# Splitting z of the first batch on GpSimd, with split scores from half step 6 and a half-wide diagonal half in the second chunk

## The chip, the cores and the metric

The kernel runs on one core of one Trainium2 chip. The core has engines that work side by side, each through its own queue of instructions in order: TensorE (PE in the profile; PEld is its loading of weights), VectorE (DVE), ScalarE (ACT), GpSimd (POOL), and SyncE (SP), which here issues all DMAs. They share the on-chip memory SBUF; PE writes its results to PSUM. The metric is the device time of one execution in microseconds (us), the median over several runs.

## The reference

Two stages, of which the change touches the first. For each of 8 batches with 2496 tokens, `u` and `v` have 256 columns and `z` has 64:

```python
scores = scale * np.matmul(z, z.transpose(0, 2, 1))   # scale = 1 / 2496
attn = np.maximum(scores, 0.0) ** 2
out = np.matmul(attn, v)
x = u * out
```

The scores are symmetric, which the kernel uses. The second stage, a mixture of experts with soft routing (slots of 8 experts filled by a softmax over all tokens, two small layers for each expert, and a second softmax that spreads the results back), takes `x` as its input.

## The kernel before

**Tiles.** The tokens of a batch are cut into 5 blocks (0 to 4) of up to 512. A chunk is the 512 queries of one block; its sums over all keys build up in PSUM (`acc`). A chunk goes through the 5 blocks of keys in the order that `MEETS` gives it (`FIRST_MEETS` for the first batch), each in two halves of 256 keys, so it has 10 half steps. The list `halves` holds all half steps of all batches, numbered from 0.

**One half step.** `scores` multiplies keys by queries on PE. `prepare` takes the result through ACT (`Relu`, then `Square`, tile `r`), and splits it in two parts, `ph` (rounded to the fast matmul format fp32r) and `pl` (what the rounding left, a subtraction on DVE). The sums are three products: `v` high with `ph`, `v` low with `ph`, `v` high with `pl`. The loop (lines 865 to 895) runs the sums of half step `h` while it prepares half step `h + 2` (from half step 18 on, `h + 3`).

**Scores, raw and split.** A raw score takes z in 32 bits as it was loaded: two matmuls, which PE works off in several passes. A split score takes z as a high and a low part (`zt`) and needs six matmuls in fp32r (line 293). Half steps below `RAW_SCORES` use raw scores. The raw z of batch 0 lies in `cw` until it is no longer needed.

**Splitting z.** `load_z` (line 103) starts the DMA of one block and returns `split`: twice a cast of 64x512 and a subtraction of 64x512. In the first batch `z_splits` holds these functions, and the loop runs them at its end (line 893) after half steps 8 to 11, as `FIRST_Z` says. Block 0 isn't split, since in half steps 0 to 9 its scores are raw and later ones are taken turned. `open_loads` issues the loads of z and v in a fixed order while a ring of four raw v tiles has room; blocks 0, 1 and 2 are issued before the loop, 3 during `prepare_first`, 4 in the loop at half step 1.

**Turned half steps.** Where a pair of blocks has met before with the roles exchanged, its scores are not computed again: at the first meeting DVE transposes `r` into `y` (32x32 blocks), `store` writes `y` to DRAM, and `fetch` reads it back rearranged. Such a half step is `turned` and goes without scores, `Relu` and `Square`. On the diagonal (a block with itself) a half can be borrowed likewise: an entry such as `(1, 0)` in `MEETS` names a single half; one with part 2 lends its transposed second half (`lend`), and the one with part 3 computes scores for only half of its queries and gets the other half from DRAM (`borrow`). In `FIRST_MEETS` the second chunk, `(1, 0, 2, 4, 3)`, has no such halves: half steps 10 and 11 are the whole diagonal, 12 and 13 are turned, 14 to 19 are blocks 2, 4 and 3.

**Order of work.** The wrapper `InOrder` pins every instruction of PE, ACT, DVE and SP behind the one written before it on its engine. Instructions that don't go through it, those of `constants` and the no-operation below, are placed by a planner where they fit.

**The no-operation on GpSimd.** When half step `h + 2` has scores to compute, the sums of `h` are cut into two phases with the scores between them. The two phases write the two halves of `acc` crosswise, and phase 1 must not begin before phase 0 has ended:

```python
if phase == 0:
    turn = nc.gpsimd.nop()   # line 484
    await_(turn, mm)
    return turn
```

The no-operation waits for the last matmul of phase 0, and the first matmul of phase 1 waits for the no-operation. Beside these GpSimd has only `constants` at the start (lines 164 to 179) and two instructions near the end (lines 916 and 918).

Of the kernel before, what the change touches and what calls it, by code (L numbers as in the profile page):

```python
# [37 lines left out]
MEETS = (  # L38
# [3 lines left out]
)  # L42
FIRST_MEETS = ((0, 1, 2, 3, 4), (1, 0, 2, 4, 3)) + MEETS[0][2:]

FIRST_Z = {8: 1, 9: 2, 10: 4, 11: 3}

RAW_SCORES = 12

PAD = 224

# [1 line left out]
def f32(ap):  # L52
    return ap.bitcast(F32)
# [14 lines left out]
def attn_soft_moe_kernel(ctx, tc, uT, v, zz, phi, ww, outT):  # L68
    nc = tc.nc

    pe, act, dve, sp = (InOrder(tc, x) for x in (nc.tensor, nc.scalar, nc.vector, nc.sync))

    def pool(st, name, n, side=None):
        return st.enter_context(
# [28 lines left out]
    def load_z(b, j):  # L103
        if b == 0:
            raw = cw[:, 19 + 4 * j : 23 + 4 * j].rearrange("p g n -> p (g n)")
        else:
            raw = raws.tile([P, 512], F32, tag="raw", name=f"zr_{b}_{j}", bufs=NRAW)
        sp.dma_start(raw, zz[b, :, j * 512 : (j + 1) * 512])
        zraw[b, j] = raw

        def split():
            t = zt[b, j]
            for h in (1, 0):
                rows = HALF[h]
                act.copy(t[rows, h], raw[rows])
                dve.tensor_sub(t[rows, 1 - h], raw[rows], f32(t[rows, h]))

        return split

# [19 lines left out]
    z_splits, v_splits = {}, []  # L139
# [24 lines left out]
    def constants():  # L164
        make_identity(nc, ident)


        nc.gpsimd.memset(rsel, 0.0)
        for h in range(4):
            rows = slice(h * NS, (h + 1) * NS)  # L170
            nc.gpsimd.tensor_copy(ssel[rows], ident[rows, rows])
        for h in range(2):
            for r in range(4):
                nc.gpsimd.tensor_copy(
                    rsel[:, h, r, 16 * h : 16 * h + 16].rearrange("k (j s) -> k j s", s=SE),
                    ident.rearrange("k (j q) -> k j q", q=NS)[:, :, 0:SE],
                )
        sp.dma_start(phi_sb, phi.rearrange("(c p) s -> p c s", p=P))
        nc.gpsimd.memset(one, 1.0)
# [11 lines left out]
    def chunks(b):  # L191
        if b < B - 1:
            return [(j, 0, min(QC, S - j * QC), b * S + j * QC) for j in range(NQ)]
        t0 = b * S
        out = [(NQ - 1, 0, ROT, t0)]
        out += [(j, 0, QC, t0 + ROT + j * QC) for j in range(NQ - 2)]
        j = NQ - 2
        return out + [(j, o, QC // 2, t0 + ROT + j * QC + o) for o in (0, QC // 2)]
# [20 lines left out]
    for b in range(B):  # L219
        for ch, meets in zip(chunks(b), MEETS[b == B - 1] if b else FIRST_MEETS, strict=True):  # L220
            order = []
# [18 lines left out]
    def run(todo):  # L240
        now, todo[:] = todo[:], []
        for f in now:
            f()
# [17 lines left out]
    def scores(k, ps=None, cut=slice(None)):  # L261
# [22 lines left out]

        if k < RAW_SCORES:
            for h, rows in enumerate(HALF):
# [168 lines left out]
    def sums_halves(k, acc, phase, before):  # L455


        x = halves[k]
        todo = [[], []]
        hi, lo = pend[k]  # L460
        for t, kt in enumerate(x.tiles):
            vt = vt_[x.b, kt // 2][:, kt % 2]
            hh, lh, hl = (vt[:, 0], hi[:, t]), (vt[:, 1], hi[:, t]), (vt[:, 0], lo[:, t])
            if kt < KT - 1:
                for h in range(2):
                    todo[h] += [hh, lh, hl]
            else:

                todo[0] += [hh] if phase else [hh, lh]
                todo[1] += [hl] if phase else [lh, hl]  # L470
        for i in range(len(todo[0])):
            for h, rows in enumerate(HALF):
                vp, pp = todo[h][i]
                c = h ^ phase ^ side[0]
                mm = pe.matmul(
                    totals(acc, c, x), vp[rows, c * P : (c + 1) * P], columns(pp[rows], x),
                    start=(x.begins and phase == 0 and i == 0),
                    stop=(x.ends and phase == 1 and i == len(todo[0]) - 1),
                )
                if before is not None:  # L480
                    await_(mm, before)
                    before = None
        if phase == 0:
            turn = nc.gpsimd.nop()
            await_(turn, mm)
            return turn
        side[0] ^= 1

    def sums_whole(k, acc):

        x = halves[k]
        hi, lo = pend[k]
        for t, kt in enumerate(x.tiles):
            assert kt < KT - 1
            vt = vt_[x.b, kt // 2][:, kt % 2]
            for c in range(2):
                for i, (l, r) in enumerate(((0, hi), (1, hi), (0, lo))):
                    pe.matmul(
                        totals(acc, c, x), vt[:, l, c * P : (c + 1) * P], columns(r[:, t], x),
                        start=(x.begins and t == 0 and i == 0),  # L500
                        stop=(x.ends and t == 1 and i == 2),
                    )
# [270 lines left out]
    def weights(left):  # L773

        if left in W_TAKES:
            W_TAKES[left]()
        for i in W_LOADS.get(left, ()):
            load_w(i)
# [26 lines left out]
    def transfers(h):  # L805

        x = halves[h]
        if x.at == 2:
            load_u(x.b, x.ch)
        for k in range(h + 1, min(h + 9, len(halves))):  # L810
            y = halves[k]

            if y.turned and y.opens and k not in arriving and k not in fetched:
                if k - h <= 7 and (y.b, y.p, y.ch[0]) in scratch:
                    fetched.add(k)
                    fetch(k)
            if y.borrows and k - h <= 5 and k not in fetched and (y.b, y.p, y.p) in scratch:
                fetched.add(k)
                borrow(k)
        for f, b, i in splits.get(h + 2, ()):  # L820
            if (b, 0) not in vt_:
                take_blocks(b)
            landing.setdefault(h + 2, []).extend([f(b, i)] if f is load_z else f(b, i))
        while stores and stores[0][0] <= h + 1:
            stores.pop(0)[1]()

    def split_first_v():
        if v_splits:
            for f in v_splits.pop(0):
                f()  # L830
            open_loads(NRAW)
# [3 lines left out]
    def between_last(k):  # L835

        if k:
            if k == 1:
                xps.append(sc_ps.tile([P, 2, QC], F32, tag="sc", name="tr_first"))
                two = [raws.tile([P, 2, D], F32, tag="raw", name=f"xt_last_{i}", bufs=NRAW) for i in range(2)]  # L840
                xt_last.extend(t[:, i] for t in two for i in range(2))
            ps = xps[0][:, k - 1, 0:D]
            turn_x(ps, xg_[NQG - 1], k - 1)
            copy_x(act.copy, ps, xt_last[k - 1])
# [16 lines left out]
    prepare(1)  # L861
    keep_busy(2)
    constants()
    acc = None
    for h, x in enumerate(halves):
        if x.begins:
            acc = acc_ps.tile([P, 2, QC], F32, tag="acc", name=f"acc_{x.ch[3]}")
        last = len(halves) - h
        transfers(h)
        weights(last)  # L870
        for f in landing.pop(h, ()):
            behind.append(f)
        if work and (x.at > 1 or last <= 20):
            work.pop(0)()
        ahead = [k for k in range(h + 2 + (h > CATCH), h + 3 + (h >= CATCH)) if k < len(halves)]
        split_first_v()
        if ahead and not halves[ahead[0]].turned:
            turn = sums_halves(h, acc, 0, None)
            prepare(ahead.pop(0))
            sums_halves(h, acc, 1, turn)  # L880
        else:
            if ahead and not x.ends:
                prepare(ahead.pop(0))
            elif not ahead:
                run(middle)
                run(behind)
                between_last(3 - last)
            sums_whole(h, acc)
        if x.ends:
            finish_chunk(x.b, x.ch, acc)  # L890
        for k in ahead:
            prepare(k)
        if h in FIRST_Z:
            z_splits.pop(FIRST_Z[h])()
        del pend[h]


# [4 lines left out]
    x = xg_.pop(q)  # L902
# [274 lines left out]
```

## Time and profile before

| | before |
|---|---|
| device time, median of 3 runs | 1358.04 us (1357.69 to 1358.5) |
| the profiled execution, device time | 1357.9 us |
| its span, first to last instruction | 1356.1 us |
| PE busy | 1334.5 us, 98% |
| DVE busy | 1083.8 us, 80% |
| ACT busy | 909.1 us, 67% |
| GpSimd busy | 3.7 us, 0% |
| DMA, share of 16 engines | 70.5% |

The page of the profile gives busy times for the whole span, and the chain of work that ended last, followed back from the last instruction. Other views give the same by groups of instructions (count, busy time, mean of one, idle time before them and what ended it), by waits, or in order of time. In a row such as `acc<-ph,v 64*128 64x512 f32 x4` the tile written stands before the arrow, the tiles read behind it; `x4` says that four equal instructions are merged. Matmuls are pipelined and their ends are modelled, so the distance between starts says more than the length of one row.

### The profile page before, as it was taken

Reading aid. Unit: us, or ns where it says so; the run is one execution under the profiler, and the core shown is the slowest. Engines: PE = TensorE matmul, PEld = TensorE weight load, DVE = VectorE, ACT = ScalarE, POOL = GpSimd, SP = SyncE. Lnnn points to the kernel's source line nnn. Section 1 sums busy time; section 2 is a strip of 40 time slices with the busy share of each in tenths; the row PEclk is TensorE's granted clock in tenths of the full one; section 3 lists DMA queues with packets and bytes.
Section 4 is the critical chain, followed back from the end, with each engine's and each line's share of the span. In section 5 each row is a group of like instructions: output and inputs, shape, how many; then the busy total and the mean of one; then the engine's idle time right before and its main releaser. Section 6 shows DMA issues by size and latency. Waiting matters only on the chain.

```text
span 1356.1 us, 27350 instructions
## 1 busy us (share of the span) xinstructions
PE 1334.5 (98%) x10927; PEld 1062.7 (78%) x10927; DVE 1083.8 (80%) x1446; ACT 909.1 (67%) x1095; POOL 3.7 (0%) x22
## 2 busy tenths in 40 slices
PE   9999999999999999999999999999999999999985
PEld 6777887778777887778877788778877788778952
DVE  7878897779868898688987889698986789866564
ACT  8866685668756787566856688566875668654453
POOL 0000000000000000000000000000000000000000
PEclk9999999999999999999999999999999999999985
DMA  7567677675759667676776676687575677769969
GB/s 225 142 195 251 202 193 231 194 245 161 219 167 302 206 154 212 182 256 203 189 228 194 229 208 172 210 265 234 150 228 172 236 235 185 215 168 302 360 273 377
DMA packets 132511, 297.28 MB, mean 219 GB/s; under 512 B 17440, under 2 KB 36896, under 8 KB 120608
## 3 DMA queue, kind: packets, MB, share of 16 engines
q1 hardware_dynamic: 132384, 295.54, 70.5%
q8 instruction: 86, 1.41, 0.4%
q14 instruction: 41, 0.34, 0.1%
HBM read 161.25 MB, written 112.98 MB: 202 GB/s over the span
## 4 chain that ended last, share of the span: by engine, by line
PE 95%; ACT 2%; DVE 1%; issue 1%; DMA 0%; SPq 0%; ACTq 0%; DVEq 0%
PE acc L64 77%; PE sc L64 11%; PE lg L64 3%; PE pf L64 2%; ACT ot L64 1%; ACT r L64 1%; PE po L64 1%; PE h L64 1%; DMA vr<-in_v 0%; DVE pl L64 0%; PE idle L64 0%; DVE z L64 0%; DVE y L64 0%; ACT v L64 0%; DVE ph L64 0%
## 5 line engine op out<-in xcount | busy, mean ns | idle before, releaser
L64 PE MATMUL acc<-ph,v 64*128 64x512 f32 (+5 forms) x5036 | 988.1, 387 | 0.6 <-ACT r L64 0.5
L64 PEld LDWEIGHTS acc<-ph,v 64*128 64x128 f32 (+1 forms) x5036 | 593.4, 185 | 147.3 <-issue 24.1
L64 PE MATMUL acc<-pl,v 64*128 64x512 f32 (+5 forms) x2518 | 622.2, 383 | 0.4 <-DVE pl L64 0.3
L64 DVE TENSOR_TENSOR pl<-r,ph 128x1024 fp32r<-128x1024 f32 (+2 forms) x413 | 468.6, 1142 | 119.9 <-ACT ph L64 110.2
L64 ACT CAST ph<-r 128x1024 fp32r<-128x1024 f32 (+1 forms) x285 | 290.3, 1023 | 110.5 <-PE acc L64 75.0
L64 ACT ACTIVATE r<-sc 128x1024 f32<-128x1024 f32 (+2 forms) x244 | 232.2, 952 | 196.7 <-PE sc L64 191.8
L64 PEld LDWEIGHTS acc<-pl,v 64*128 64x128 f32 (+1 forms) x2518 | 306.7, 185 | 60.8 <-DVE pl L64 2.3
L64 ACT ACTIVATE r<-r 128x1024 f32<-128x1024 f32 (+2 forms) x245 | 241.2, 985 | 7.0
L64 DVE STREAM_TRANSPOSE y<-r 128x1024 f32<-128x1024 f32 x160 | 198.0, 1238 | 0.0
L64 PE MATMUL sc<-z,z 64*128 64x512 f32 x912 | 131.4, 393 | 0.2 <-ACT r L64 0.2
L64 DVE CAST ph<-r 128x1024 fp32r<-128x1024 f32 (+2 forms) x128 | 76.1, 595 | 40.4 <-ACT r L64 36.6
L64 PEld LDWEIGHTS sc<-z,z 64*128 64x128 f32 x912 | 85.0, 184 | 20.8 <-ACT r L64 0.6
L64 ACT CAST z<-zr 64x512 fp32r<-64x512 f32 x70 | 43.3, 619 | 48.8 <-DMA zr<-in_zz 47.5
L64 DVE TENSOR_TENSOR xg<-acc,ut 128x1024 f32<-128x1024 f32 (+7 forms) x57 | 48.4, 872 | 34.4 <-PE acc L64 34.4
L64 DVE TENSOR_TENSOR z<-zr,z 64x512 fp32r<-64x512 f32 x70 | 48.1, 687 | 16.4 <-ACT z L64 14.4
L64 DVE TENSOR_TENSOR v<-vr,v 128x512 fp32r<-128x512 f32 x80 | 53.5, 669 | 8.9 <-ACT v L64 8.9
L64 ACT CAST v<-vr 128x512 fp32r<-128x512 f32 x78 | 47.8, 613 | 17.3 <-DMA vr<-in_v 17.3
L64 PE MATMUL sc<-z 64*128 64x512 f32 (+1 forms) x468 | 54.6, 339 | 0.0
L64 DVE STREAM_TRANSPOSE y<-xg 128x512 f32<-128x512 f32 x72 | 49.5, 688 | 0.0
L64 PEld LDWEIGHTS sc<-z 64*128 64x128 f32 x468 | 41.2, 185 | 7.6
L64 DVE COPY ot<-pf 128x1024 f32<-128x1024 f32 (+2 forms) x22 | 24.3, 1103 | 22.8 <-PE pf L64 22.8
L64 ACT COPY ot<-pf 128x1024 f32<-128x1024 f32 (+2 forms) x22 | 20.1, 915 | 26.8 <-PE pf L64 26.8
(151 smaller groups left out, 481.3 us busy)
## 6 DMA issues: line engine op xcount, KB each, us to landing
turned<-y SPq DMA_DIRECT2D x320, 256.0 KB, 4.4
r<-turned SPq DMA_DIRECT2D x76, 1024.0 KB, 6.3
xt<-y SPq DMA_DIRECT2D x288, 72.0 KB, 3.4
vr<-in_v SPq DMA_DIRECT2D x80, 256.0 KB, 3.7
outT<-ot SPq DMA_DIRECT2D x16, 1024.0 KB, 5.7
ut<-in_uT SPq DMA_DIRECT2D x31, 512.0 KB, 5.3
zr<-in_zz SPq DMA_DIRECT2D x35, 256.0 KB, 5.2
lent<-yd SPq DMA_DIRECT2D x132, 64.0 KB, 2.2
```

What stands on the lines that cost most here:

```text
L64: return lambda *a, **k: self.tc.keep_in_program_order(f(*a, **k))
```

## The change

Three things change in the first batch, and nothing else does:

- All five blocks of z are split, in the order 0, 2, 3, 4, 1, on GpSimd instead of ACT (casts) and DVE (subtractions). The splits are issued at the beginning of a half step of the loop, as soon as the block's load has been issued: blocks 0, 2 and 3 at half step 0, blocks 4 and 1 at half step 2. A wrapper `gps` pins each behind what was written before it on GpSimd.
- Scores are raw below half step 6 instead of 12.
- The second chunk's order becomes `((1, 0), 0, 2, 4, 3, (1, 1))`: half step 10 is the diagonal's first half and lends, 11 and 12 are turned, 13 to 18 are blocks 2, 4 and 3, and 19 is the diagonal's second half, which borrows.

```diff
-FIRST_MEETS = ((0, 1, 2, 3, 4), (1, 0, 2, 4, 3)) + MEETS[0][2:]
-
-FIRST_Z = {8: 1, 9: 2, 10: 4, 11: 3}
-
-RAW_SCORES = 12
+FIRST_MEETS = ((0, 1, 2, 3, 4), ((1, 0), 0, 2, 4, 3, (1, 1))) + MEETS[0][2:]
+
+FIRST_Z = 0, 2, 3, 4, 1
+
+RAW_SCORES = 6
...
-    pe, act, dve, sp = (InOrder(tc, x) for x in (nc.tensor, nc.scalar, nc.vector, nc.sync))
+    pe, act, dve, sp, gps = (
+        InOrder(tc, x) for x in (nc.tensor, nc.scalar, nc.vector, nc.sync, nc.gpsimd)
+    )
...
-                act.copy(t[rows, h], raw[rows])
-                dve.tensor_sub(t[rows, 1 - h], raw[rows], f32(t[rows, h]))
+                (gps.tensor_copy if b == 0 else act.copy)(t[rows, h], raw[rows])
+                (dve if b else gps).tensor_sub(t[rows, 1 - h], raw[rows], f32(t[rows, h]))
...
-    acc = None
+    acc, first_z = None, list(FIRST_Z)
     for h, x in enumerate(halves):
+        while first_z and first_z[0] in z_splits:
+            z_splits.pop(first_z.pop(0))()
...
-        if h in FIRST_Z:
-            z_splits.pop(FIRST_Z[h])()
```

## The prediction

> **What bounds the kernel now.** I read the page first: the span, the busy times, and the chain that ended last.
>
> ```profile
> span 1356.1 us, 27350 instructions
> ...
> PE 1334.5 (98%) x10927; PEld 1062.7 (78%) x10927; DVE 1083.8 (80%) x1446; ACT 909.1 (67%) x1095; POOL 3.7 (0%) x22
> ...
> PE 95%; ACT 2%; DVE 1%; issue 1%; DMA 0%; SPq 0%; ACTq 0%; DVEq 0%
> ```
>
> TensorE (PE) is busy for 98% of the span and carries 95% of the chain, so a saving has to come out of PE's own work or out of its few waits. GpSimd (POOL) does nothing in the loop. Next I read the chain in order of time over the first 60 us, where the change acts (columns: start, length, what).
>
> ```profile
> 19.76 0.86 PE sc L64 x4
> 20.62 2.81 PE acc L64 x24
> ...
> 27.09 0.89 PE sc L64 x4
> 28.00 1.04 ACT r L64
> ...
> 47.46 0.69 DVE z L64
> 48.18 0.68 DVE z L64
> 48.87 1.15 DVE pl L64
> 50.06 1.20 PE acc L64 x8
> 51.26 0.70 PE sc L64 x6
> 51.97 2.79 PE acc L64 x24
> ```
>
> The reader is to see two things. A half step is scores (sc) and then sums (acc): raw scores take 0.86 us, split scores 0.70, the sums 2.8 either way. And from 28 us the chain leaves PE for ACT and DVE and ends in the subtractions of the z splits, after which PE starts again at 50.06. The timeline shows what that restart costs:
>
> ```profile
> 49.00 0.73 PE L64 MATMUL acc<-ph,v 64*128 64x512 f32 x4
> 50.06 0.50 PE L64 MATMUL acc<-pl,v 64*128 64x512 f32 x2 [0.33 <-DVE pl L64]
> 50.40 0.63 PE L64 MATMUL acc<-ph,v 64*128 64x512 f32 x4
> 50.87 0.40 PE L64 MATMUL acc<-pl,v 64*128 64x512 f32 x2
> ```
>
> Undisturbed, the pl row starts 0.47 us after the ph row before it (50.40 to 50.87); here it came 1.06 later. That is 0.6 us lost, the one stall between 9 and 60 us that the change can remove.
>
> **Part 1, PE's work.** Half steps 6 to 10 change from raw to split scores: 5 x (0.86 - 0.70) = 0.80 us saved. The diagonal's second half was raw half step 11, 0.86. It becomes half step 19 with half the queries. The trace has the like of it in the next chunk:
>
> ```profile
> 99.20 0.36 PE sc L64 x6
> ```
>
> So 0.86 - 0.36 = 0.50 saved. The turned half steps move from 12 and 13 to 11 and 12 and the others from 14-19 to 13-18; they keep their work. Together **1.30 us**, all of it on PE and so on the path.
>
> **Part 2, what leaves ACT and DVE.** The grouped view of the first 60 us has both:
>
> ```profile
> L64 DVE TENSOR_TENSOR z<-cw,z 64x512 fp32r<-64x512 f32 x8 | 5.5, 687 | 0.2
> L64 ACT CAST z<-cw 64x512 fp32r<-64x512 f32 x8 | 5.0, 619 | 0.2
> ```
>
> 5.0 us leave ACT and 5.5 leave DVE, out of the very stretch that made the stall. I count **0.6 us** for the stall. What is late next are the products of the turned half steps, which ACT and DVE then make without the z work between; I cost that at nothing, and at up to 0.6 if the moved fetch were late. The fetch is `r<-turned`:
>
> ```profile
> 26.11 0.34 SPq L64 DMA_DIRECT2D r<-turned  x1
> ```
>
> It went out at 26.11 and is needed at about 41 us in the new order; its issue moves one half step forward in SP's queue, past no load of v (the last leaves at 23.04 in the row below). If SP stands there until the store has landed, it stands before stores of y, which nobody needs for 20 us.
>
> ```profile
> 23.04 0.46 SPq L64 DMA_DIRECT2D vr<-in_v  x1
> ```
>
> The half-wide half adds a half-size transpose on DVE, four stores and a load:
>
> ```profile
> 85.32 0.71 DVE L64 STREAM_TRANSPOSE yd<-r 128x512 f32<-128x512 f32 x1
> ```
>
> 0.71 us on DVE, at about 40 us, stands against the 5.5 that leave; the DMAs have nine half steps to pass through DRAM. Cost nothing; without that cover 0.7.
>
> **Part 3, what GpSimd gets.** Twenty instructions: per tile of z two casts and two subtractions of 64x512, now for five tiles (z of block 0 wasn't split before). The trace has no such instruction on GpSimd. Nearest rows:
>
> ```profile
> L174 POOL COPY rsel<-ident 128x16 f32<-128x16 f32 x8 | 1.1, 188 | 0.1
> L916 POOL MEMSET tiny<- 128x512 f32 x1 | 0.5, 527 | 1270.1 <-PE xt L64 1270.1
> L918 POOL TENSOR_SCALAR tiny<-ssel 128x128 f32<-128x128 f32 x1 | 0.3, 297 | 0.0
> ```
>
> A cast lies between 0.53 (a write of 512 columns) and 1.19 (four times the 128 columns of L918). I take 0.6, near the row with the same number of columns. A subtraction reads two inputs: between 0.53 and 2.4 (L918, four times the columns, twice the inputs); I take 1.2. A tile then takes 3.6 us (bounds 2.1 and 7.2), five tiles 18 us (10.6 to 36). GpSimd is free from 3.7 us. z of block 3 is issued late and lands 3.9 us after, by the median of its queue rows:
>
> ```profile
> 9.24 0.42 SPq L64 DMA_DIRECT2D cw<-in_zz  x1
> ...
> cw<-in_zz SPq DMA_DIRECT2D x5, 256.0 KB, 3.9
> ```
>
> So tiles 0, 2 and 3 are done by about 13.1 + 3.6 = 17 us, and 4 and 1 by about 25. The split scores of half step 6 start near 23.3, of 8 near 30, of 10 near 37. The covers are 6 us and more, so the splits themselves cost PE nothing.
>
> In the opening DVE has no room:
>
> ```profile
> 7.56 0.30 PEld L64 LDWEIGHTS acc<-ph,v 64*128 64x128 f32 x4 [0.60 <-DVE ph L64]
> 8.29 0.18 PEld L64 LDWEIGHTS acc<-pl,v 64*128 64x128 f32 x2 [0.43 <-DVE pl L64]
> ```
>
> PE waits for DVE there, and GpSimd's reads of the same memory now run beside it. The trace shows no moment with both at work, so the price is open: nothing if they don't meet, 5 us if they exclude each other (below), and not below nothing, since GpSimd takes over no work of the opening. I take one GpSimd subtraction in front of DVE, **1.2 us**.
>
> **The sum:** -1.30 - 0.6 + 1.2 = -0.7 us. The profiled execution took 1357.9 us for a span of 1356.1; the median of the runs is 1358.04. So the forecast is **1357.3 us**, for a profiled span near 1355.4.
>
> **Rival 1, slower: DVE and GpSimd exclude each other.** Place: 3.7 to 37.7 us. If an instruction of DVE with two inputs, or one of its casts, and an instruction of GpSimd can't run at once, the time has to hold both. These rows are the window from 3.7 to 12 and DVE's groups from 12 to 37.7:
>
> ```profile
> 3.70:12.00 8.30, 7.67 (x56) 4.64 (x56) 7.09 (x15) 7.49 (x15) 0.01 (x1) 1.00 0.76 253
> ...
> L64 DVE STREAM_TRANSPOSE y<-r 128x1024 f32<-128x1024 f32 x7 | 8.7, 1238 | 0.0
> L64 DVE TENSOR_TENSOR pl<-r,ph 128x1024 fp32r<-128x1024 f32 x7 | 8.6, 1226 | 4.3 <-ACT ph L64 4.2
> L64 DVE TENSOR_TENSOR v<-vr,v 128x512 fp32r<-128x512 f32 x7 | 4.8, 684 | 0.0
> L64 DVE CAST ph<-r 128x1024 fp32r<-128x1024 f32 x2 | 1.3, 652 | 0.0
> ```
>
> In the opening DVE leaves 8.30 - 7.09 = 1.2 us. After it, subtractions and casts take 8.6 + 4.8 + 1.3 = 14.7 of 25.7 us and leave 11.0, most of it under transposes. That is 12.2 us of room for 18 us of GpSimd. The margin with which DVE is ahead of PE is small:
>
> ```profile
> 31.23 1.23 DVE L64 TENSOR_TENSOR pl<-r,ph 128x1024 fp32r<-128x1024 f32 x1 [0.68 <-ACT ph L64]
> 33.32 0.40 PE L64 MATMUL acc<-pl,v 64*128 64x512 f32 x2
> ```
>
> The product is done at 32.46 and read at 33.32: 0.9 us. So 18 - 12.2 - 0.9 = 4.9 us reach PE, and the time is 1358.04 - 1.9 + 4.9 = 1361.0. It decides against the change once the five tiles take more than 12.2 + 0.9 + 1.9 = 15 us. With the low bound of 10.6 it costs nothing; with tiles of 4.5 us it is 1365.5. Against it: ACT and DVE read the same memory side by side all through this trace without stretching. For it: DVE's cast of 1024 columns takes 0.65 us and the subtraction 1.23, as if the cast drew on a second path. The Trainium skill, "SBUF — State Buffer", section "Who interferes with whom", says that GpSimd shares a port pair with DVE, that it is an exclusive lock, and that a DVE instruction with two SBUF inputs contends with a GpSimd instruction that reads SBUF. No run here shows that yet; by that rule this rival is the case, and the time is the 1361.0 just worked out.
>
> **Rival 2: POOL's queue.** Between the two phases of a half step PE waits for a no-operation on POOL (line 484), and POOL works in order:
>
> ```profile
> PEld acc L64 <- POOLq L484: 2.4, 10, 0.2
> ```
>
> Ten times 0.24 us, hidden under the scores, which run 0.86; some 0.6 us of the cover is left. Behind a z instruction that waits for its tile or for the cast before it, the no-operation is late, then PE's second phase, then all that follows. One instruction of 1.2 us in front costs 0.6, in five half steps 3.0: 1358.04 - 1.9 + 3.0 = 1359.1; if z of block 3, landing at 13.1, stands in front of the first one, due at 9, it is 4 us more: 1363. For it: five half steps' worth of GpSimd work in one queue. Against it: nothing ties the no-operation to the splits but its place in the queue.
>
> **Rival 3: the split z isn't there** when half step 6 wants it. With tiles at the bound of 7.2 us, tile 3 is ready near 26 instead of 23.3, and 4 and 1 follow at 33 and 40 for 30 and 37: 3 us, 1358.04 - 1.9 + 3 = 1359.1.
>
> **How the numbers follow.** Forecast 0.42 (1356.1 without any clash to 1358.6), rival 1 0.30 (1358.5 to 1365.5), rival 2 0.17 (1358 to 1363), rival 3 0.07; 0.04 for a gain beyond the sum, which would need more than the 1.9 us that I can find. 0.2% is 2.7 us, about what a measurement of this kernel can tell from no change: the bounds are 1355.3 and 1360.8. Slower takes 0.20 of rival 1, 0.11 of rival 2 and 0.04 of rival 3; faster 0.05; the rest, 0.60, is same. The range is 1355.8 to 1363.5; over it lies the far end of rival 1. Forecast and rivals lie on both sides; the forecast's own range is 1356.1 to 1358.6.
>
> **What would show it.** Right: score rows of 0.70 from half step 6 on and 0.36 for half step 19, no wait for DVE near 50 us, PE's first loop rows within 1.2 us of their old places, DVE's subtractions at 1.23. Rival 1: DVE or GpSimd rows stretched, or gaps on DVE with no releaser, while GpSimd works. Rival 2: PE's wait for L484 above 0.24. Rival 3: scores that wait for POOL. If PE loses more than 2 us before 40 us, the step "one subtraction in front of DVE" was wrong.

## The result, and the profile after

The changed kernel takes 1373.07 us (median of 4 runs, 1369.29 to 1373.71) against 1358.27 us for the kernel before (4 runs, 1357.69 to 1358.93). The ratio is 1.0103, 95% interval 1.0091 to 1.0115 (the quotient of the two medians is 1.0109): it is slower by 14.8 us, more than the top of the forecast range allowed.

The page of the changed kernel, with the span, the busy times and the engines' shares of the chain that ended last:

```profile
span 1370.8 us, 27388 instructions
...
PE 1334.7 (97%) x10939; PEld 1066.7 (78%) x10939; DVE 1085.4 (79%) x1440; ACT 903.4 (66%) x1088; POOL 26.4 (2%) x42
...
PE 95%; DMA 2%; ACT 1%; DVE 1%; POOL 0%; issue 0%; SPq 0%; ACTq 0%; DVEq 0%; POOLq 0%
```

PE's busy time is as before to 0.2 us, in a span that is 14.7 us longer. A lower sum was forecast; part of what was saved is hidden by stretches at half clock, further down. DMA has come into the chain with 2%, where it had 0%, but most of that is far from the change: in order of time the chain holds two stores of the output near the end, 7.0 us each, and two loads of the first 30 us, 2.97 and 4.98. So the page alone doesn't say where the time goes. The view of waits says more. PE's largest wait in the first 60 us of the changed kernel (what waits, for whom, us in total, times, longest) is:

```profile
PE acc L64 <- POOLq L486: 9.5, 2, 7.9
```

L486 is the no-operation on GpSimd. Where the rest goes is read from the timeline of the changed kernel's PE: the rows of raw scores begin a new half step each (2, 3, 4, 5), the others carry PE's waits in brackets, the last is the first row of the logits.

```profile
8.79 0.72 PE L64 MATMUL acc<-ph,v 64*128 64x512 f32 x4 [2.30 <-ACT r L64]
...
11.32 1.14 PE L64 MATMUL acc<-ph,v 64*128 64x512 f32 x4 [1.57 <-DVE ph L64]
...
12.93 1.91 PE L64 MATMUL sc<-cw 64*128 64x512 f32 x4
...
17.54 1.03 PE L64 MATMUL sc<-cw 64*128 64x512 f32 x4
...
20.18 0.73 PE L64 MATMUL acc<-ph,v 64*128 64x512 f32 x4 [1.61 <-POOLq L486]
...
23.09 1.02 PE L64 MATMUL sc<-cw 64*128 64x512 f32 x4
...
32.01 1.22 PE L64 MATMUL acc<-ph,v 64*128 64x512 f32 x4 [7.89 <-POOLq L486]
...
36.40 1.04 PE L64 MATMUL sc<-cw 64*128 64x512 f32 x4
...
97.80 1.09 PE L64 MATMUL lg<-xg,phi_sb 64*32 64x256 f32 x32
```

The first row names ACT and is to be read with care: what the sums read there is `ph`, and DVE's second cast of it ends at 8.65, 0.1 before PE starts; ACT's rows had run on without it. It is a wait for DVE. In the kernel before, the scores of half steps 2 and 5 and the logits are

```profile
8.63 1.02 PE L64 MATMUL sc<-cw 64*128 64x512 f32 x4
...
19.60 1.02 PE L64 MATMUL sc<-cw 64*128 64x512 f32 x4
...
82.52 1.09 PE L64 MATMUL lg<-xg,phi_sb 64*32 64x256 f32 x32
```

and those of half steps 3 and 4 start at 12.27 and 15.94. The lag is thus 4.3 us at half step 2, 5.3 at 3, 7.2 at 4, 16.8 at 5, and 15.3 at the logits. After half step 5 the change gives back 1.5 us; before it, it loses 16.8, in two places.

**The opening, 4.3 us.** The timeline of the changed kernel from 4.4 to 8.4 us, GpSimd and DVE:

```profile
4.48 1.32 POOL L64 TENSOR_TENSOR z<-cw,z 64x512 fp32r<-64x512 f32 x1
...
4.71 1.64 DVE L64 TENSOR_TENSOR v<-vr,v 128x512 fp32r<-128x512 f32 x1
...
6.90 1.26 POOL L64 TENSOR_TENSOR z<-cw,z 64x512 fp32r<-64x512 f32 x1
...
7.00 1.45 DVE L64 TENSOR_TENSOR pl<-r,ph 128x256 fp32r<-128x256 f32 x1
```

A DVE row that begins inside a GpSimd subtraction ends somewhat less than its own undisturbed length after that subtraction: the `v` row (0.69 alone) at 6.35, 0.55 after 5.80; the `pl` row (0.42 alone) at 8.45, 0.29 after 8.16. The two don't share, they take turns. PE's first sums start at 8.79 instead of 6.44, the next at 11.32 instead of 7.56. A row of 0.42 us becomes one of 1.45, since it starts 0.1 after a GpSimd row of 1.26. In the groups of DVE from 3.7 to 24 us (count, busy time, mean ns, idle) the changed kernel has

```profile
L64 DVE TENSOR_TENSOR v<-vr,v 128x512 fp32r<-128x512 f32 x5 | 4.8, 956 | 0.0
L64 DVE CAST ph<-r 128x512 fp32r<-128x512 f32 x3 | 3.4, 1131 | 0.0
...
L64 DVE TENSOR_TENSOR pl<-r,ph 128x256 fp32r<-128x256 f32 x2 | 1.9, 935 | 0.1
...
L64 DVE STREAM_TRANSPOSE y<-r 128x1024 f32<-128x1024 f32 x1 | 1.2, 1231 | 0.0
```

where the kernel before has

```profile
L64 DVE TENSOR_TENSOR v<-vr,v 128x512 fp32r<-128x512 f32 x6 | 4.1, 685 | 0.0
...
L64 DVE CAST ph<-r 128x512 fp32r<-128x512 f32 x3 | 1.3, 423 | 0.1
L64 DVE TENSOR_TENSOR pl<-r,ph 128x256 fp32r<-128x256 f32 x2 | 0.8, 424 | 0.1
```

Subtractions take 1.4 and 2.2 times as long, casts 2.7 times; the transpose, with one input and no cast, stays, at 1231 ns for 1237.

**The queue of GpSimd, 1.6 + 7.9 us.** The chain that ended last, in order of time, in the changed kernel (start, length, what; `SPq` and `POOLq` are instructions of SP and GpSimd that don't count as busy, here the issue of a transfer and the no-operation):

```profile
19.52 1.10 DVE v L64
...
20.64 0.33 SPq L64
...
21.02 4.98 DMA cw<-in_zz
...
26.05 0.62 POOL z L64
...
31.28 0.61 POOL z L64
...
31.94 0.03 POOLq L486
```

It is to be read backwards. PE's second phase of half step 2, at 32.01, waits for the no-operation; that stands in GpSimd's queue behind the splits of block 4 and the first cast of block 1; the first of these waits for block 4's load, which SP issues at 21.02, because a `v` tile of the ring comes free only when DVE's subtraction ends at 20.62. Before the change that load's issue began at 15.22 and ended at 16.81. So the delay of the opening comes back in the queue as a later load, and the queue hands it to PE.

**Half clock.** The view by windows (length; busy time and count of PE, PEld, DVE, ACT, POOL; granted clock; DMA share; GB/s) of the changed kernel:

```profile
11.30:15.00 3.70, 3.68 (x14) 1.93 (x16) 3.66 (x5) 0.11 (x1) 2.12 (x2) 0.54 0.26 73
...
32.00:35.50 3.50, 3.50 (x18) 2.79 (x20) 0.00 (x0) 0.00 (x0) 3.11 (x3) 0.52 0.86 305
```

After each of the two idle stretches PE is busy, but at a granted clock of 0.54 and 0.52: at most 1.7 us lost each time (3.68 x 0.46, 3.50 x 0.48). From half step 4 to 5 the lag grows by 9.65: 7.89 of wait and about 1.7 of half clock.

### The profile page after: what moved, and what is told of

Its sections match the earlier page's. It is cut to its first block, busy times and chain, and to the rows that moved or that the text cites. A ratio compares the mean times of both kernels' runs of the same rounds, so it can differ in the third digit from the quotient of the medians.

```text
span 1370.8 us, 27388 instructions
## 1 busy us (share of the span) xinstructions
PE 1334.7 (97%) x10939; PEld 1066.7 (78%) x10939; DVE 1085.4 (79%) x1440; ACT 903.4 (66%) x1088; POOL 26.4 (2%) x42
## 4 chain that ended last, share of the span: by engine, by line
PE 95%; DMA 2%; ACT 1%; DVE 1%; POOL 0%; issue 0%; SPq 0%; ACTq 0%; DVEq 0%; POOLq 0%
PE acc L64 78%; PE sc L64 11%; PE lg L64 3%; PE pf L64 1%; DMA outT<-ot 1%; PE po L64 1%; ACT ot L64 1%; ACT r L64 1%; PE h L64 1%; POOL z L64 0%; DMA cw<-in_zz 0%; DVE v L64 0%; DVE ot L64 0%; DMA vr<-in_v 0%; DVE ph L64 0%
## 5 line engine op out<-in xcount | busy, mean ns | idle before, releaser
L64 PE MATMUL sc<-z,z 64*128 64x512 f32 x936 | 135.0, 393 | 0.2 <-ACT r L64 0.2
```

The costliest lines, as they stand in the source:

```text
L64: return lambda *a, **k: self.tc.keep_in_program_order(f(*a, **k))
```

## The experiments

Two theories were held against each other and against both being at work. **Queue**: the no-operation behind the z work makes the time. **Port**: DVE and GpSimd keep each other from running, and DVE is late for PE. Each ratio is against the kernel before, run beside it on the same chip (medians of 1357.98 to 1358.18 us).

### One pair at a time, behind the no-operation: e1_pairs

```diff
-FIRST_Z = 0, 2, 3, 4, 1
+FIRST_Z = 0, 3, 4, 1, 2
...
-        while first_z and first_z[0] in z_splits:
-            z_splits.pop(first_z.pop(0))()
...
             turn = sums_halves(h, acc, 0, None)
+            split_pair()
...
             sums_whole(h, acc)
+            split_pair()
```

`split_pair` puts one cast and one subtraction into GpSimd's queue.

> The changed kernel, with z still split on GpSimd, but one cast and one subtraction per half step, put into GpSimd's queue behind the no-operation of that half step, in the order of blocks 0, 3, 4, 1, 2 (nothing in the opening, nothing that waits for a load in front of a no-operation). Queue theory (PE's loss is its wait for the no-operation behind GpSimd's z work): the waits of 1.6 and 7.9 us vanish. If that were all, the opening's delay of 4.3 us would stay; it is an effect of GpSimd's z work beside DVE, so by the port theory (DVE and GpSimd exclude each other) it vanishes too because nothing runs there, and DVE rows that meet a pair are stretched in ten half steps instead: 1.9 us of GpSimd per half step, of which 1.2 fit under a transpose. Sum 1358.3 - 1.9 + 0 to 5 us: 1356.4 if DVE's margin of 0.9 us and the transposes take it, 1361 if each pair costs 0.7 us beyond them. Rival (the loss is due to the moved fetch and the new order of the second chunk, not to GpSimd): stays near 1372.

1362.26 us, 1.0031 [1.0019, 1.0043]: 10.8 us less than the change, and 1.3 more than the upper end of what was expected. PE no longer waits for the no-operation. What remains is DVE. Waits of PE in the first 60 us, then the groups of DVE from 3.7 to 50 us:

```profile
PE acc L64 <- DVE pl L64: 3.8, 5, 1.3
```

```profile
L64 DVE TENSOR_TENSOR pl<-r,ph 128x1024 fp32r<-128x1024 f32 x9 | 14.4, 1602 | 0.4
L64 DVE TENSOR_TENSOR v<-vr,v 128x512 fp32r<-128x512 f32 x10 | 10.5, 1055 | 0.0
```

Nine subtractions at 1602 ns instead of 1226 and ten at 1055 instead of 685: 3.4 + 3.7 = 7.1 us more work for DVE, whose rows no longer have idle time between them. The transposes beside them stay at 1232 ns. This is the loss by the port without the queue, and outside the opening.

### The no-operation on ScalarE: e2_nop_on_act and e8_before_nop_on_act

```diff
-            turn = nc.gpsimd.nop()
+            turn = nc.scalar.nop()
```

> The changed kernel with the no-operation between the two phases on ScalarE instead of GpSimd; GpSimd's z work is as in the changed kernel. Queue theory: PE no longer waits for GpSimd, so of the 14.8 us the 1.9 lost before half step 4's scores and the 9.7 lost before half step 5's go, 1373.1 - 11.6 = 1361.5, as far as ScalarE's own queue doesn't hold the no-operation up. Port theory: the opening is as late as in the changed kernel, scores of half step 2 near 12.9 us instead of 8.6, and DVE rows stretched as there. If the port alone made the loss, the time stays near 1373.

> The kernel before with the no-operation on ScalarE throughout. If ScalarE's queue holds the no-operation up in the steady state, it is 6 to 8 us slower than before, 1364 to 1366, which is the part of the earlier run's time that has nothing to do with the change; if not, 1358.2.

The changed kernel with this edit takes 1371.45 us, 1.0103 [1.0088, 1.0119], as much as without it. By that alone the queue theory would have fallen. But its logits start at 87.90 us instead of 97.80, so it is 9.9 us ahead there and loses that later. The kernel before with the same edit shows why: 1365.51 us (2 runs), 1.0055 [1.0037, 1.0073], 7.5 us slower, though its logits are only 0.7 us late. The no-operation has moved into a queue with work in it; from 110 to 1240 us the weight loads wait for it there:

```profile
PEld acc L64 <- ACTq L484: 7.2, 13, 0.7
```

So e2 mixed two things: it took away the queue's cost in the first batch and added another of about the same size in all later batches. In the first ten half steps e8's score rows are 3.66 us apart as before, so an edit confined to these would be clean.

### The no-operation on ScalarE in the first ten half steps only: e5_nop_on_act_first

```diff
-            turn = nc.gpsimd.nop()
+            turn = (nc.scalar if k < 10 else nc.gpsimd).nop()
```

> The changed kernel with the no-operation on ScalarE in the first chunk alone (half steps 0 to 9), on GpSimd from then on. By the logits of the first 1024 tokens the run with ScalarE throughout was 9.9 us ahead of the changed kernel (87.7 against 97.6 us); it lost the lead later, where GpSimd has no z work, so by the queue theory that later loss is the price of ScalarE's own queue and goes here: 1373.1 - 9.9 = 1363.2. If the lead is lost again, something else in the changed kernel costs time later, and the total stays near 1371.

1363.98 us, 1.004 [1.0026, 1.0053]: 9.1 us less than the change. The waits of PE in the first 60 us no longer name POOLq, and those that are left are DVE's (the first, named after ACT, as in the changed kernel):

```profile
PE acc L64 <- ACT r L64: 2.7, 1, 2.7
PE acc L64 <- DVE ph L64: 1.7, 1, 1.7
PE acc L64 <- DVE pl L64: 1.1, 4, 0.5
```

### GpSimd only writes: e3_gpsimd_writes_only

```diff
-                (gps.tensor_copy if b == 0 else act.copy)(t[rows, h], raw[rows])
-                (dve if b else gps).tensor_sub(t[rows, 1 - h], raw[rows], f32(t[rows, h]))
+                if b == 0:
+                    gps.memset(f32(t[rows, h]), 0.0)
+                    for _ in range(2):
+                        gps.memset(f32(t[rows, 1 - h]), 0.0)
+                    continue
+                act.copy(t[rows, h], raw[rows])
+                dve.tensor_sub(t[rows, 1 - h], raw[rows], f32(t[rows, h]))
```

> The changed kernel with each z cast on GpSimd replaced by one write of a constant, and each subtraction by two (so GpSimd reads no SBUF; the split z of the first batch is zero, and with it all split scores of that batch). Port theory, reads: DVE's subtractions in the opening run at 0.69 (128x512) and 0.42 (128x256) again, and scores of half step 2 come near 8.6 us; if the write side is shared too, DVE's casts (0.28 and 0.42 alone) are still stretched. Queue theory: no instruction in GpSimd's queue waits for a load or for the one before it, so PE's waits of 1.6 and 7.9 us vanish; what stays is a no-operation behind a few writes of 0.5 us, under 2 us in all. Time 1356.4 to 1359.

1362.81 us, 1.003 [1.0016, 1.0045]: 10.3 us less than the change, but 3.8 more than the upper end of what was expected. GpSimd is busy for 16.8 us with 30 writes, where the ten casts and ten subtractions would take 18.7 undisturbed. Groups of DVE from 3.7 to 24 us:

```profile
L64 DVE TENSOR_TENSOR v<-vr,v 128x512 fp32r<-128x512 f32 x6 | 4.1, 685 | 0.0
...
L64 DVE CAST ph<-r 128x512 fp32r<-128x512 f32 x3 | 1.9, 635 | 0.0
```

The subtractions are back at 685 ns although GpSimd works beside them. So it is GpSimd's reading that stops a subtraction of DVE. Casts stay stretched, 635 for 423 ns, by writes alone. The wait for the no-operation is still there, 3.9 us in two pieces, the longest 3.0 instead of 7.9, behind writes that follow each other from 9.82 us on. That it is shorter has a second reason beside the port: a write doesn't need the raw z, so GpSimd no longer waits for loads at all, while in the changed kernel it does so for 6.1 us, 4.3 of them for block 4. This run thus takes away the reads and the waits for loads together.

The Trainium skill, "SBUF — State Buffer", section "Who interferes with whom", has both halves of this: a DVE instruction with two SBUF inputs contends with a GpSimd instruction that reads, not with one that only writes, and DVE's casts can take the shared pair as a whole. These runs agree (956 against 685 ns; 635 against 423 ns).

### Both taken away: e9_both_removed

The edits of e3 and e5 together.

> The changed kernel with both causes taken away: GpSimd writes constants instead of splitting z (one write for a cast, two for a subtraction; split z of the first batch is zero), and the no-operation of half steps 0 to 9 is on ScalarE. If GpSimd's queue and the shared reads are the whole loss, what stays is the prediction's gain of 1.9 us less what the writes still cost VectorE's casts in the opening (scores of half step 2 came 0.9 us late in the run with writes alone): 1356.3 to 1357.5. If a third cause is at work (the fetch, the turned order, split scores), it stays above 1358.2.

1356.9 us (11 runs, 1356.54 to 1358.2), 0.9993 [0.9984, 1.0002]. Of the waits of PE in the first 60 us there remain

```profile
PE acc L64 <- DVE ph L64: 0.5, 1, 0.5
```

and the first 0.8 us before PE's first instruction. With e3, e5 and the change this makes a square, in us:

| | GpSimd reads | GpSimd only writes |
|---|---|---|
| no-operation on GpSimd | 1373.07 (the change) | 1362.81 (e3) |
| no-operation on ScalarE, first ten half steps | 1363.98 (e5) | 1356.9 (e9) |

From left to right GpSimd's reads go, and with them its waits for loads; from top to bottom the queue goes out of PE's way. The first step is worth 10.3 us above and 7.1 below, the second 9.1 on the left and 5.9 on the right. Below, PE waits neither for the no-operation nor for a split, so 7.1 is the price of the port alone, less what the writes still cost in e9 (scores of half step 2 at 9.66 for 8.63). On the right no load is waited for, so 5.9 is the price of a queue that holds work but no load. The two are both at work, and 3.2 us of the loss belong to neither alone. Two things in the changed kernel can make them: its queue waits for loads, one of them made late by the opening (the chain above), and its GpSimd rows are themselves stretched by DVE, 22.7 us for 18.7. How much each makes isn't shown, and with the four runs of the change spread over 4.4 us the 3.2 is itself a rough figure. The split scores of e9 are computed from zeros, but follow each other 3.49 us apart as in the change. Nothing else of any size remains.

### The half-wide half alone: e4_half_wide

```diff
-FIRST_MEETS = ((0, 1, 2, 3, 4), (1, 0, 2, 4, 3)) + MEETS[0][2:]
+FIRST_MEETS = ((0, 1, 2, 3, 4), ((1, 0), 0, 2, 4, 3, (1, 1))) + MEETS[0][2:]
```

> The kernel before with only the second chunk's new order (half step 10 lends, 19 borrows and is half wide); raw scores below 12, z split on ScalarE and VectorE after half steps 8 to 11 as before. By the prediction's sum: one raw score of 0.86 us less and one of 0.36 more, 0.5 us less: 1357.8. If the moved fetch or the extra transpose costs PE anything, 1358.3 or more, with a wait for the fetch or for DVE near 45 us.

1357.98 us, 1.0 [0.9992, 1.0009]. Timeline of this kernel (DVE, and the PE row with its wait):

```profile
43.85 1.41 DVE L64 TENSOR_TENSOR z<-cw,z 64x512 fp32r<-64x512 f32 x2
...
46.32 1.21 DVE L64 TENSOR_TENSOR pl<-r,ph 128x1024 fp32r<-128x1024 f32 x1
...
47.58 0.49 PE L64 MATMUL acc<-pl,v 64*128 64x512 f32 x2 [1.07 <-DVE pl L64]
```

The half step is shorter for PE, but DVE has a z split, the end of a chunk and a product to do in it; PE waits 1.07 us. The 0.5 us are not gained as long as DVE splits z at this place.

### Late pairs on GpSimd: e6_late_pairs

The change with scores raw below 12 as before, blocks 1, 2, 4, 3 only, and one pair on GpSimd in each half step from 7 on, away from the opening and the loads.

```diff
-FIRST_Z = 0, 2, 3, 4, 1
-RAW_SCORES = 6
+FIRST_Z = 1, 2, 4, 3
+RAW_SCORES = 12
...
+    def split_pair(h):
+        if first_z and h >= 7:
+            j, i = first_z.pop(0)
+            z_splits[j]((i,))
```

> The changed kernel with raw scores below half step 12, block 0 not split, and one cast and one subtraction per half step on GpSimd from half step 7 on, blocks 1, 2, 4, 3, each behind that half step's no-operation. Port theory: fewer of VectorE's rows meet them, since half steps 10 to 12 have less for VectorE to do; the loss is below the 5.9 us of the early pairs, 8 pairs at up to 0.6 us each less what the vanished z work on VectorE gives back: 1356.8 to 1360. Queue theory alone: 1358.2 - 0.5 (half-wide half) - 0.6 (the stall near 50 us) = 1357.1.

1360.46 us, 1.0014 [1.0005, 1.0023]: still 2.5 us slower. From the timeline:

```profile
39.41 1.28 POOL L64 TENSOR_TENSOR z<-cw,z 64x512 fp32r<-64x512 f32 x1
...
39.85 1.40 DVE L64 CAST ph<-r 128x1024 fp32r<-128x1024 f32 x1
...
41.30 0.74 PE L64 MATMUL acc<-ph,v 128*128 128x512 f32 x2 [0.96 <-DVE ph L64]
...
41.79 2.15 POOL L64 TENSOR_TENSOR z<-cw,z 64x512 fp32r<-64x512 f32 x1
...
42.85 0.50 PE L64 MATMUL acc<-pl,v 128*128 128x512 f32 x1 [0.81 <-DVE pl L64]
```

A cast of 0.65 takes 1.40 behind GpSimd, and at once PE waits. Of the eight pairs only those near 41 and 43 us make PE wait, 0.96 and 0.81 us, but from 43.5 to 47.0 PE then runs at a granted clock of 0.51. The clash doesn't need the opening; it costs where DVE's lead over PE is smaller than what one clash adds.

### The splits on ACT and DVE at the change's places: e7_z_on_act_dve

```diff
-                (gps.tensor_copy if b == 0 else act.copy)(t[rows, h], raw[rows])
-                (dve if b else gps).tensor_sub(t[rows, 1 - h], raw[rows], f32(t[rows, h]))
+                act.copy(t[rows, h], raw[rows])
+                dve.tensor_sub(t[rows, 1 - h], raw[rows], f32(t[rows, h]))
```

> The changed kernel with the z splits at the same places in the order (half steps 0 and 2) but on ScalarE and VectorE as before. GpSimd theory (both parts): no wait for GpSimd and no stretched row, but 3 tiles at half step 0 put 3.7 us on ScalarE and 4.1 on VectorE in front of later work, 2 more at half step 2, with 0.9 us of margin; ScalarE's queue also stands until the load of block 3 has landed: 5 to 9 us lost, 1.9 gained, 1361 to 1366. If what hurts is only that the splits come so early, it is as slow as the changed kernel, near 1373.

1365.84 us, 1.0057 [1.0044, 1.0071]: 7.2 us less than the change, without GpSimd. The waits, first 110 us:

```profile
PE sc L64 <- ACT r L64: 6.0, 2, 3.2
...
ACT z L64 <- DMA cw<-in_zz: 4.1, 2, 3.5
```

The place is bad for ACT and DVE too: here ACT stands before a cast whose block hasn't landed, and `Relu` behind it.

### Half a block at a time on ACT and DVE: e10_spread, e11_spread_late, e12_spread_in_time

Three tries at keeping the gain: the kernel before with the half-wide half and with the splits of a block cut in two, at the ends of half steps of their own (half step: block, half).

```diff
-FIRST_Z = {8: 1, 9: 2, 10: 4, 11: 3}
+FIRST_Z = {1: (1, 1), 3: (1, 0), 5: (2, 1), 7: (2, 0), 11: (4, 1), 12: (4, 0), 13: (3, 1), 14: (3, 0)}  # e10
+FIRST_Z = {6: (1, 1), 8: (1, 0), 9: (2, 1), 10: (2, 0), 11: (4, 1), 12: (4, 0), 13: (3, 1), 14: (3, 0)}  # e11
+FIRST_Z = {1: (1, 1), 3: (1, 0), 5: (2, 1), 7: (2, 0), 8: (4, 1), 9: (4, 0), 10: (3, 1), 11: (3, 0)}     # e12
```

> The kernel before with the half-wide half, and z split on ScalarE and VectorE as before, but half a block at a time: block 1 after half steps 1 and 3, block 2 after 5 and 7, block 4 after 11 and 12, block 3 after 13 and 14. It tests the part of the prediction that a stall near 50 us goes when z work leaves that stretch: 1358.2 - 0.5 - 0.6 = 1357.1, if 0.62 us on ScalarE and 0.69 on VectorE in every second half step fit into the 0.3 us that a half step leaves plus the 0.9 of margin. If they don't, PE waits for VectorE between 12 and 37 us and the time is 1358 or more.

> As the run before, but block 1 after half steps 6 and 8, block 2 after 9 and 10. The z work of blocks 1 and 2 then still meets the turned half steps near 45 us, so the stall there stays at 1 us or more: 1358, as the half-wide half alone gave.

> The spread z work of the earlier run on ScalarE and VectorE, with blocks 4 and 3 brought forward to half steps 8 to 11 (in the two spread runs they came after 11 to 14, and PE waited up to 3.3 us for them; that was an error of the experiment, not a property of the half-wide half). If only that was wrong, the waits for z are gone and the time is between 1357.0 (the half-wide half and no stall near 45 us) and 1358.0 (the stall as with the half-wide half alone). Above 1359 would mean that z work on VectorE in half steps 1 to 7 doesn't fit.

e10: 1367.71 us, 1.0074 [1.006, 1.0087]; e11: 1368.79 us, 1.0081 [1.0067, 1.0094]. In both I had put blocks 4 and 3 too late: with the second chunk one half step shorter their scores come earlier, and PE waits for the split, against what was expected of both (first 110 us of e10; 1.5 us more are waits for ACT's cast of z):

```profile
PE sc L64 <- DVE z L64: 4.6, 2, 2.9
```

e12 mends that: 1358.63 us, 1.0004 [0.9995, 1.0013], no change. PE still waits for DVE in three places near 41, 44 and 48 us (0.25, 0.59 and 0.47 us), which eats the half step's 0.5. No version tried is measurably faster than the kernel before.

## Why the prediction was wrong

- **"One GpSimd subtraction in front of DVE, 1.2 us" failed first.** In place of 1.2 us the clash with DVE cost 7.1 (e5 against e9), and the queue of the no-operation, for which the sum held nothing, 5.9 to 9.1. The text named its own test: more than 2 us lost by PE before 40 us. PE had lost 4.3 at 12.9. The step took one clash for the whole opening; but DVE's rows there follow each other without a gap while GpSimd's do the same, so DVE lost a turn to nearly each GpSimd instruction that began beside it, and half clock followed. e3 shows that it is the reads: without them subtractions are at 685 ns.
- **Rival 1** had the mechanism, and the rule of the skill named beside it was the case. Its size was off: 4.9 us reaching PE, measured 7.1. The sum let DVE use up all free room before PE would pay. But the room lies in the wrong places: PE pays on the spot where a clash adds more than DVE's lead (0.75 us on the cast in e6), and may then run for 3.5 to 6.8 us at half clock, which no term held.
- **Rival 2** had the mechanism too, and was mis-sized: 3.0, or 7 with a load in front, measured 5.9 to 9.1. It looked for the load of block 3 in front of the first no-operation. That cost 1.61 us, with the second. The dear one was block 4's load in front of the third, 7.89, since SP could issue that load only at 21.02.
- **The two were treated as alternatives.** Each had a chance and a time of its own, and the range ended at 1363.5, about where either alone lands (1362.81 and 1363.98). They act through different resources, a memory port and a queue, so nothing kept both from coming true; together they cost some 3 us more than the sum of the two alone. With the sizes as forecast, both together would have given 1364 to 1368. This, more than any single term, put the result out of range.
- **"The splits themselves cost PE nothing" and rival 3:** right in what they weighed. No score of the first batch waits for GpSimd; split z was always there in time. But the cover was counted only up to the scores, not up to the no-operation that shares the queue. The finish times were early too: tiles 4 and 1 were to be done by about 25, and were done at 31.2 and 35.2. That working had no term for block 4's load, whose issue ended at 16.81 even in the kernel before.
- **GpSimd's own prices were right:** cast 0.6 forecast, 0.61 measured; subtraction 1.2 forecast, 1.26 measured, where they run alone. In place they average 0.88 and 1.40, and twenty of them take 22.7 us instead of 18, since GpSimd is also held up by DVE.
- **Parts 1 and 2, -1.9 us together:** the sizes hold where the trace shows them, split scores at 0.70 and the last half at 0.35:

```profile
40.23 0.70 PE sc L64 x6
...
83.80 0.35 PE sc L64 x6
```

  From half step 5 to the logits, after the last wait for the no-operation, the changed kernel gains 1.5 us on the kernel before. With both causes taken away, e9 is 1.2 us faster than the kernel before by the medians, from 2.2 faster to 0.3 slower by the interval. That fits 1.9, and can't be told from nothing.

What stays open: how the loss of the opening divides between the clash itself and the half clock after it, since no kernel had the one without the other. That the remaining gain is real isn't shown either.

## What to carry to other kernels

Ask of each pair of rivals whether one excludes the other; where they act through different resources, their prices add, and the range must hold the sum. Before work goes on an idle engine, list what else stands in its queue: an instruction that computes nothing but passes a turn on makes the whole queue part of the critical path, with each load that the work waits for. And an engine that reads the memory beside DVE is not free because it is idle: find where DVE is least ahead of PE, and price the clash there.

## What the runs showed of the hardware

- **DVE and GpSimd take turns by whole instructions.** A DVE row of 0.42 us becomes 1.45 behind a GpSimd subtraction of 1.26, and a GpSimd subtraction of 1.26 becomes 2.15 behind DVE (e6). DVE's transposes run through undisturbed at 1.23.
- **PE's clock fell to half after waits shorter than I had thought to matter.** In the changed kernel two waits of 2.30 and 1.57 us within the opening were followed by a granted clock of 0.54; in e5, with waits of 2.70 and 1.66, the window from within the second wait on was

```profile
10.40:17.20 6.80, 5.13 (x18) 2.98 (x20) 5.46 (x8) 1.33 (x2) 2.16 (x3) 0.52 0.27 82
```

  that is 6.8 us at half clock. In e6 two waits of 0.96 and 0.81 us were enough: between 40 and 43 us PE was busy for 1.23 of 3 us, and from 43.5 to 47.0 the clock was 0.51. In e1, whose longest wait is 1.32 us, it stayed at 1.00 up to 60 us, also after waits of 0.65 and 0.60 close together. So the longest wait doesn't decide by itself; what does, these runs don't show. The Trainium skill, "TensorE: Matmul & The Clock Gate", section "Why this matters for your kernels", asks for no idle gaps above about 3 us; here gaps below that, close to each other, were enough.
- **A no-operation has the price of its queue.** On idle GpSimd it takes 0.24 us and hides; behind the z splits PE waited 1.61 and 7.89 us for it; on ScalarE, in the kernel before, it made the time 7.5 us longer. The queue holds both ways: in the changed kernel a no-operation that waited for PE kept GpSimd's next subtraction back by 1.58 us.
